# A state-space scan and a feed-forward with PReLU on one core: one layout for all chunk pairs, and another order of the first loads

## The chip, the cores and the metric

The kernel runs on one core of a Trainium2 chip. The metric is the device time in microseconds of one execution. The median of three runs before the change is 359.67 us (358.67 to 361.34). A profile shows one execution: its engines are PE (TensorE, the matmuls; PEld is its weight load), DVE (VectorE), ACT (ScalarE), POOL (GpSimd) and SP (SyncE, which here only issues DMAs). All data is 32-bit floating point.

## What is computed

Two steps, the second fed with the first one's output:

```python
# x: (4, 8, 768, 32)  a: (4, 8, 768)  B, C: (4, 8, 768, 16)
for c in range(nc):                       # chunks of the sequence
    cum = np.cumsum(la, axis=-1)          # la = log(clip(a, 1e-6, 1)) of the chunk
    L = np.exp(cum[..., :, None] - cum[..., None, :]) * causal
    y_intra = np.einsum('bhij,bhjd->bhid', (Cc @ Bc.T) * L, xc)
    y_inter = np.einsum('bhin,bhnd->bhid', Cc, state) * np.exp(cum)[..., None]
    y[:, :, sl] = y_intra + y_inter
    state = decay_full * state + sum_j(B_j x_j * decay_from_j)
# bridge: y as 3072 tokens of 256
h = x @ w_in                              # 256 -> 2048
g = np.maximum(h, 0.0) + alpha * np.minimum(h, 0.0)
out = g @ w_out                           # 2048 -> 256
```

The weights come as 64-bit numbers and are turned into 32-bit ones on the chip ("conversion" below: each of 16 pieces passes ScalarE, GpSimd, VectorE and GpSimd again).

## The kernel before

The sequence is cut into chunks of 128 tokens (Q), six to a batch element. Chunks go in pairs, twelve in all (NP); two pairs make a group of 512 tokens (GC chunks, GT tokens), and the feed-forward works by group. The order of the work is written out by hand: each engine executes its instructions in the order of the program, and a DMA is issued in the order of its queue (SP's, and ScalarE's for a few).

Per pair there are five kinds of work. **Loads**: B, C and x as tokens on the partitions (`nat`, `xt`), the running product of a for each chunk (`ap`, later `pf`), and the decay rows spread over the partitions (`abc`), which come from device memory (`scratch`), where `rows_out` stores the clamped rows (`z`) and their running products (`pf`). **Turning** B and C so that heads and states lie on the partitions (`bc`): by TensorE transposes and a ScalarE copy for pairs 0 to 4 (L640, L807), by one block transpose of VectorE for later ones (L545), whose data comes in blocks (L209). **Decays**: scans on VectorE along the tokens (`dec`), from `abc` or, for pairs 0 and 1, from rows that TensorE spreads from `ap` and `a1` (L499, L511). **Gram**: C times B (L713, L702, L822), multiplied into `dec` on VectorE (L724). C is first multiplied by `par`, which keeps even or odd heads (`cz`). **Output and state**: the new state is the old one times the decay plus B'x (`added`, L600, L831; in halves L589), masked by head on GpSimd (`sm`); y is the state times the decayed C (L768, L870; L750) plus `dec` times x (L776, L878; L758), copied to `xT` by ScalarE.

There are two layouts. Pairs 0 to 5 (`gp < HALF`) keep each chunk on all 128 partitions, and TensorE works with 128 rows of x and tiles of 128 columns. Pairs 6 to 11 put chunk k on half k of the partitions (64 tokens at a time, `SQ` = 192 columns of decay per head for both chunks), so that the two chunks' matmuls use different quarters of the array and the part above the diagonal is left out; the state products of the other half of heads need their operands on the other half of the partitions (`shifted`).

Pairs 0 and 1 are written out in `first_two`, interleaved with the conversion of the first weight pieces. `hidden_two` (L1011) is the feed-forward of the first four hidden blocks, two at a time, by halves of 256 tokens; then a loop over f from 4 to 15 takes 512 tokens at once (`hidden`, L996; `output`, L1034), with pairs 2 and 3 between, and after it 20 `quad` steps (L1120, L1095) do groups 1 to 5 by a scheme of seven products, with the later pairs between them. `keep_warm` (L326) is filler: matmuls whose result is not used.

Of the kernel before, what the change touches and what calls it, by code (L numbers as in the profile page):

```python
# [9 lines left out]
F32 = mybir.dt.float32  # L10
# [12 lines left out]
def kernel(  # L23
# [47 lines left out]
    WARM = 8  # L71
# [8 lines left out]
    HALF = NP // 2  # L80
# [9 lines left out]
    lda = ctx.enter_context(tc.tile_pool(name="lda", bufs=3))  # L90
# [48 lines left out]
    def load_tokens(dst, src, t0):  # L139


        d = dst.rearrange("p j (h w) -> p j h w", h=H)
        for k in range(2):
            for j in range(2):
                t = t0 + k * Q + j * HQ
                nc.sync.dma_start(out=d[HQ * k : HQ * (k + 1), j],
                                  in_=src[:, t : t + HQ, :].rearrange("h p w -> p h w"))

    def load_spread(gp, b, c):

        for w, t in enumerate(loads["p", gp][1] if gp >= HALF else ()):
            rows = scratch["z", b // 2].rearrange("(b h c) t -> b c h t", b=2, h=H)
            for k in range(2):
                nc.sync.dma_start(
                    out=t[HQ * k : HQ * (k + 1), : 4 * SQ].rearrange("p (h t) -> p h t", h=4),
                    in_=rows[b % 2, c + k, 4 * w : 4 * w + 4].unsqueeze(0)
                    .to_broadcast([HQ, 4, SQ]))
        for k, t in enumerate(loads["p", gp][1] if gp < HALF else ()):
            rows = scratch["z", b // 2].rearrange("(b h c) t -> b c h t", b=2, h=H)[b % 2, c + k]
            nc.sync.dma_start(out=t.rearrange("p (h t) -> p h t", h=H),  # L160
                              in_=rows.unsqueeze(0).to_broadcast([P, H, Q]))

    def load_pair(gp, decays=True):


        b, c = divmod(2 * gp, CPB)
        turned = gp > GC
        nat = ldx.tile([P, 3, 2, H * N], F32, name="nat")
        xt = ldx.tile([P, 2, HD], F32, name="xt")

        ap = ldx.tile([P, 2 * Q], F32, name="ap")
        if gp == 0:
            load_a(ap, b, c)
        elif gp >= NB:
            rows = scratch["pf", b // 2].rearrange("(b h c) t -> b h (c t)", b=2, h=H)
            rows = rows[b % 2, :, c * Q : (c + 2) * Q]
            nc.sync.dma_start(out=ap, in_=rows.unsqueeze(1).to_broadcast([H, N, 2 * Q]))
        if gp == 0:
            load_rows(0, nc.scalar)
            nc.sync.dma_start(out=al_n, in_=moe_alpha.rearrange("(k p) -> k p", p=P))  # L180
        abc = []
        later = []
        if gp >= HALF:
            load_tokens(nat[:, 0], B[b], c * Q)
        for k in range(2 if gp < HALF else 0):
            ts = slice((c + k) * Q, (c + k + 1) * Q)
            for i, src in enumerate((B,) if turned else (B, C)):
                nc.sync.dma_start(out=nat[:, i, k].rearrange("p (h n) -> p h n", h=H),  # L188
                                  in_=src[b, :, ts, :].rearrange("h p n -> p h n"))

            def load_x(k=k, ts=ts):
                nc.sync.dma_start(out=xt[:, k].rearrange("p (h d) -> p h d", h=H),
                                  in_=x[b, :, ts, :].rearrange("h p d -> p h d"))

            if gp < NB:
                later.append(load_x)
            else:
                load_x()
        for load_x in later:
            load_x()  # L200
        if gp == 0:
            loads["a", 1] = prep.tile([P, 2 * Q], F32, name="a1")
            load_a(loads["a", 1], b, c + 2)
        for i, src in enumerate((B, C) if turned else ()):


            for e in range(2):
                first = src[b, e : e + 1, c * Q : (c + 2) * Q, :]
                nc.sync.dma_start(out=nat[:, 1 + e, i],  # L209
                                  in_=bass.AP(tensor=first.tensor, offset=first.offset,  # L210
                                              ap=[[2 * S * N, P // 32], [8 * N, 32], [1, 8 * N]]))
        for k in range(2 if gp >= NB else 0):
            abc.append(lda.tile([P, H * Q], F32, name="abc"))
        loads["p", gp] = nat, abc, xt, ap
        if gp >= HALF:
            load_tokens(xt, x[b], c * Q)
        if decays:
            load_spread(gp, b, c)

    def load_second():  # L220

        rows = scratch["pf", 0].rearrange("(b h c) t -> b h (c t)", b=2, h=H)
        nc.sync.dma_start(out=loads["p", 1][3], in_=rows[0, :, 2 * Q : 4 * Q].unsqueeze(1)
                          .to_broadcast([H, N, 2 * Q]))

    al_n = const.tile([NF, P], F32, name="al_n")
    load_pair(0)
# [95 lines left out]
    def keep_warm(to, n, cols=2 * Q):  # L323

        for i in range(n):
# [6 lines left out]
    ident_h = const.tile([P, H * Q], F32, name="ident_h")  # L332
    nc.vector.tensor_copy(out=ident_h.rearrange("p (h t) -> p h t", h=H),
                          in_=ident.unsqueeze(1).to_broadcast([P, H, Q]))
# [12 lines left out]
    nc.gpsimd.tensor_tensor(out=hmask, in0=hmask, in1=bmask[:, P:], op=ALU.add)  # L347
    zeros = const.tile([P, Q], F32, name="zeros")
    nc.gpsimd.memset(zeros, 0.0)
# [46 lines left out]
    def halve_identity():  # L396

        for s in range(2):
            nc.scalar.copy(
                out=ident_p[0][HQ:].rearrange("p (a s t) -> p s a t", a=2, s=2)[:, s],  # L400
                in_=ident[HQ:, HQ * (1 - s) : HQ * (2 - s)].unsqueeze(1).to_broadcast([HQ, 2, HQ]))

    def rows_swapped():

        prs = prep.tile([RW, Q], F32, name="rpf")
        for h in range(2):
            nc.scalar.copy(out=prs[:, HQ * h : HQ * (h + 1)],
                           in_=held["pr"][:, HQ * (1 - h) : HQ * (2 - h)])
        held["prs"] = prs

    def rows_clamp(i):
        rows = loads.pop(("r", i))
        d0 = prep.tile([RW, SQ], F32, name="r0")
        nc.vector.tensor_scalar(out=d0[:, :Q], in0=rows, scalar1=1e-6, scalar2=1.0,
                                op0=ALU.max, op1=ALU.min)
        if i:
            nc.vector.tensor_scalar(out=d0[:, Q + 1 :], in0=rows[:, HQ + 1 :], scalar1=1e-6,
                                    scalar2=1.0, op0=ALU.max, op1=ALU.min)
        held[i] = d0

# [9 lines left out]

    def rows_out(i):


        d0 = held.pop(i)[:, : SQ if i else Q]
        rpf = prep.tile([RW, Q], F32, name="rpf")
        nc.vector.tensor_tensor_scan(out=rpf, data0=d0[:, :Q], data1=zeros[:RW], initial=1.0,
# [6 lines left out]
    def rows_turn(i, pr):  # L443
# [8 lines left out]
        if i == 0:  # L452
            nc.scalar.copy(out=t, in_=ps[:, :RW])
# [7 lines left out]
        if i == 0:  # L461
            nc.scalar.copy(out=alpha, in_=ps[:, RW : RW + NF])
# [978 lines left out]
```

## Time and profile before

| | us |
|---|---|
| median of three runs | 359.67 |
| the profiled execution | 359.9 |
| its span, first to last instruction | 358.2 |
| TensorE matmul busy | 350.5 |
| VectorE, ScalarE, GpSimd busy | 239.9, 173.8, 205.4 |

The first group's feed-forward starts at 17.77 us (first half of its tokens) and 24.76 us (second half), the loop over f at 28.69, the first quad at 78.96. Busy time of TensorE is modelled at the ends of matmuls, since these overlap; starts are exact. A row of the profile names a line of the kernel, the engine, the operation, the tile written and the tiles read, the shapes, the count, the busy time and the mean of one; then the idle time of the engine before it and what ended it. A line of a helper stands for all its callers.

### The profile page before, as it was taken

The numbers are of one execution on the slowest core, as the hardware profiler recorded it, in microseconds if no ns is written. First come the engines' busy times: TensorE is split into PE (matmuls) and PEld (weight loads), VectorE is DVE, ScalarE is ACT, GpSimd is POOL, SyncE is SP. The second block draws the span as 40 slices with busy tenths as digits, with TensorE's granted clock in tenths as the row PEclk, the third lists the DMA queues.
The fourth block names the chain that finished last, engine by engine and source line by source line (L and its number), as shares of the span: only waits on it lengthen the run. The fifth ranks groups of instructions, "written<-read, shape, count | busy, mean of one in ns | idle before, by whom it ended". The sixth has DMA issues, their size and how long they took to land.

```text
span 358.2 us, 7528 instructions
## 1 busy us (share of the span) xinstructions
PE 350.5 (98%) x2878; PEld 288.3 (80%) x2878; DVE 239.9 (67%) x466; ACT 173.8 (49%) x386; POOL 205.4 (57%) x222
## 2 busy tenths in 40 slices
PE   8899999999999999999999999999999999999994
PEld 8676665578788788888888888888888888888883
DVE  6987986998748756857647847757847533654272
ACT  3577666535356346346246345345445343444330
POOL 4876568589939755725655725646726544632521
PEclk9999999999999999999999999999999999999999
DMA  6989999608255403403513413413001002002003
GB/s 110 182 186 303 326 198 258 140 17 176 88 98 118 94 2 76 102 2 88 92 30 85 79 48 79 89 41 73 1 4 29 0 2 31 0 2 30 0 15 77
DMA packets 105453, 30.19 MB, mean 84 GB/s; under 512 B 79864, under 2 KB 101320, under 8 KB 105416
## 3 DMA queue, kind: packets, MB, share of 16 engines
q1 hardware_dynamic: 104488, 29.45, 37.2%
q8 instruction: 23, 0.38, 0.5%
q10 hardware_dynamic: 928, 0.25, 0.3%
q14 instruction: 14, 0.11, 0.1%
HBM read 26.32 MB, written 3.37 MB: 83 GB/s over the span
## 4 chain that ended last, share of the span: by engine, by line
PE 92%; SPq 3%; DMA 1%; DVE 1%; issue 1%; ACT 1%; POOLq 0%
PE bank L1095 34%; PE hp L1120 28%; PE bank L1034 8%; PE hp L996 6%; PE ss L1120 6%; SPq L188 2%; PE hp L1011 2%; PE ss L758 1%; PE ss L702 1%; DMA nat<-in_C_dram 1%; PE ss L750 1%; PE ss L776 1%; PE ss L713 1%; PE ss L589 1%; PE ss L768 0%
## 5 line engine op out<-in xcount | busy, mean ns | idle before, releaser
L1177 POOL TENSOR_TENSOR gt<-gt 128x512 f32<-128x512 f32 x58 | 74.1, 1277 | 21.1 <-DVE gt L1105 16.3
L1095 PE MATMUL bank<-gt,w_out 128*128 128x256 f32 x320 | 83.5, 381 | 0.0
L1095 PEld LDWEIGHTS bank<-gt,w_out 128*128 128x128 f32 x320 | 60.1, 190 | 9.2 <-issue 1.0
L1105 DVE SCALAR_TENSOR_TENSOR gt<-hp,s_mul,gt 128x256 f32<-128x256 f32 x96 | 42.0, 479 | 29.0 <-ACT gt L1103 26.8
L1167 POOL TENSOR_TENSOR gt<-gt 128x512 f32<-128x512 f32 x20 | 25.4, 1269 | 62.6 <-DVE gt L1105 57.2
L1095 PE MATMUL bank<-gt,ws 128*128 128x256 f32 x240 | 59.5, 379 | 0.0
L1103 ACT ACTIVATE gt<-hp,s_alpha 128x256 f32<-128x256 f32 x96 | 40.3, 471 | 34.5 <-PE hp L1120 31.4
L1095 PEld LDWEIGHTS bank<-gt,ws 128*128 128x128 f32 x240 | 45.6, 190 | 6.2
L1120 PE MATMUL hp<-xs,w_in 128*128 128x256 f32 x160 | 41.9, 384 | 0.0
L1120 PE MATMUL hp<-xs,ws 128*128 128x256 f32 x160 | 41.1, 380 | 0.0
L1146 DVE TENSOR_TENSOR hp<-hp,u 128x512 f32<-128x512 f32 x20 | 14.0, 699 | 35.8 <-ACT u L1144 35.8
L1120 PEld LDWEIGHTS hp<-xs,ws 128*128 128x128 f32 x160 | 30.3, 190 | 4.3 <-POOL xs L1075 0.2
L1120 PEld LDWEIGHTS hp<-xs,w_in 128*128 128x128 f32 x160 | 29.7, 190 | 4.5
L1034 PE MATMUL bank<-w_out,gt 128*128 128x256 f32 x128 | 31.0, 384 | 0.0
L1034 PEld LDWEIGHTS bank<-w_out,gt 128*128 128x128 f32 x128 | 23.6, 190 | 6.5 <-issue 3.1
L1120 PE MATMUL ss<-xT,w_in 128*128 128x256 f32 x96 | 24.6, 379 | 0.0
L996 PE MATMUL hp<-xT,w_in 128*128 128x512 f32 x48 | 22.7, 596 | 0.2 <-DVE gt L1023 0.2
L616 POOL TENSOR_TENSOR sm<-state,bmask 128x256 f32<-128x256 f32 (+1 forms) x10 | 6.2, 617 | 29.0 <-DVE state L613 29.0
L532 DVE TENSOR_TENSOR_SCAN dec<-abc,bank 128x192 f32<-128x192 f32 x48 | 22.6, 522 | 0.0
L1135 ACT COPY m<-hp 128x512 f32<-128x512 f32 x8 | 4.7, 586 | 35.7 <-PE hp L1120 35.7
L1144 ACT COPY u<-hp 128x512 f32<-128x512 f32 x20 | 11.7, 585 | 19.4 <-PE hp L1120 19.4
L1105 DVE SCALAR_TENSOR_TENSOR gt<-c,s_mul,gt 128x256 f32<-128x256 f32 x40 | 20.6, 555 | 0.0
(201 smaller groups left out, 609.6 us busy)
## 6 DMA issues: line engine op xcount, KB each, us to landing
abc<-z SPq DMA_DIRECT2D x24, 192.0 KB
raw<-in_moe_w_in_dram SPq DMA_DIRECT2D x8, 512.0 KB
raw<-in_moe_w_out_dram SPq DMA_DIRECT2D x8, 512.0 KB
abc<-z SPq DMA_DIRECT2D x8, 512.0 KB
out_dram<-o_sb SPq DMA_DIRECT2D x32, 64.0 KB
nat<-in_B_dram SPq DMA_DIRECT2D x26, 64.0 KB
nat<-in_C_dram SPq DMA_DIRECT2D x24, 64.0 KB
xt<-in_x_dram SPq DMA_DIRECT2D x12, 128.0 KB
```

What stands on the lines that cost most here:

```text
L188: nc.sync.dma_start(out=nat[:, i, k].rearrange("p (h n) -> p h n", h=H), in_=src[b, :, ts, :].rearrange("h p n -> p h n"))
L532: nc.vector.tensor_tensor_scan(out=dv[:, o : o + SQ], data0=abc[k][:, s : s + SQ], data1=ident_p[0][:, :SQ], initial=0.0, op0=ALU.mult, op ...
L996: nc.tensor.matmul(hp, w_in[:, k, f * P : (f + 1) * P], xts[g][:, k], start=(k == 0), stop=(k == KC - 1))
L1034: nc.tensor.matmul(pos[0][t // 2][:, t % 2], gt[:, t * Q : (t + 1) * Q], w_out[:, f], start=(f == 0 and t % 2 == 0), stop=(f == NF - 1), s ...
L1095: nc.tensor.matmul(ms[g][i][:, h], w, blocks[g, z][n][:, p], start=(q == 0 and h == 0), stop=(q == NQ - 1), skip_group_check=True)
L1103: nc.scalar.mul(o[:, p], h[:, p], s_alpha[:, fs[p]])
L1105: nc.vector.scalar_tensor_tensor(out=o[:, p], in0=h[:, p], scalar=s_mul[:, fs[p]], in1=o[:, p], op0=ALU.mult, op1=ALU.max)
L1120: nc.tensor.matmul(to[:, p], w(2 * z + p), b, start=start and p == 0, stop=True, skip_group_check=True)
L1144: nc.scalar.copy(out=u2, in_=A)
L1146: nc.vector.tensor_tensor(out=Y, in0=Y, in1=u2, op=ALU.add)
L1167: nc.gpsimd.tensor_tensor(out=tc_, in0=g22, in1=g12, op=ALU.subtract)
L1177: eng.tensor_tensor(out=o, in0=x0, in1=x1, op=ALU.subtract)
```

## The change

- Pairs 0 to 5 take the layout of pairs 6 to 11; the old layout's code is gone (`HALF`, `halve_identity`, `rows_swapped`, `spread`, the first form of `added`). `rows_turn` writes both halves of the partitions by four matmuls. In pairs 2 and 3 the gram comes ahead of the state sums.
- The first pair's B and C are loaded in blocks and turned by VectorE; its B is loaded as tokens too. These B loads are issued on ScalarE's queue. Pairs 1 to 4 are turned by TensorE as before.
- The second pair's decay rows come from `scratch` (`z1`), by one DMA after `rows_out`, in place of loading a again (`a1`) and clamping it.
- In `first_two`: the rows are clamped on GpSimd, the fillers are gone but for six at the start (`WARM`), the second weight piece is converted after pair 0's outputs, and loads have another order.

The core of the diff:

```diff
-    WARM = 8
+    WARM = 6
-    lda = ctx.enter_context(tc.tile_pool(name="lda", bufs=3))
+    lda = ctx.enter_context(tc.tile_pool(name="lda", bufs=2))
+    def load_blocks(nat, i, src, t0, eng=nc.sync):
+        for e in range(2):
+            first = src[e : e + 1, t0 : t0 + 2 * Q, :]
+            eng.dma_start(out=nat[:, 1 + e, i],
+                          in_=bass.AP(tensor=first.tensor, offset=first.offset,
+                                      ap=[[2 * S * N, P // 32], [8 * N, 32], [1, 8 * N]]))
+    def load_heads(dst, key, b, c):
+        rows = scratch[key, b // 2].rearrange("(b h c) t -> b h c t", b=2, h=H)
+        rows = rows[b % 2, :, c : c + 2].rearrange("h c t -> h (c t)")
+        nc.sync.dma_start(out=dst, in_=rows.unsqueeze(1).to_broadcast([H, N, dst.shape[1]]))
+    def load_first():
+        nat, _, xt, ap = pair_tiles(0)
+        load_a(ap, 0, 0)
+        load_rows(0, nc.scalar)
+        load_blocks(nat, 1, C[0], 0)
+        load_blocks(nat, 0, B[0], 0, nc.scalar)
+        load_tokens(nat[:, 0], B[0], 0, eng=nc.scalar)
+        load_tokens(xt, x[0], 0, (0,))
...
     def spread_rows(z):
         ts = [bank(r) for r in range(4)]
+        for e in range(2):
+            for r in range(4):
+                rs = slice(32 * r, 32 * r + 32)
+                row = 32 * r + N * e
+                for k in range(2):
+                    nc.tensor.matmul(ts[r][HQ * k : HQ * (k + 1), e * SQ : (e + 1) * SQ],
+                                     ident[rs, row : row + 1].to_broadcast([32, HQ]), z[rs, k],
+                                     start=e == 0, stop=True, tile_position=(32 * r, HQ * k),
+                                     skip_group_check=True)
...
         sp = spread_rows(z0)
         pr = rows_scan(0)
+        rows_product(0)
+        rows_ends(0, nc.gpsimd)
         rows_out(0)
+        load_tokens(xt0, x[0], 0, (1,))
+        load_heads(z1.rearrange("p k t -> p (k t)"), "z", 0, 2)
+        nc.sync.dma_start(out=al_n, in_=moe_alpha.rearrange("(k p) -> k p", p=P))
+        load_next()
+        nat1, _, xt1, pf1 = pair_tiles(1)
+        load_chunks(nat1[:, 1], C[0], 2 * Q)
+        load_tokens(nat1[:, 0], B[0], 2 * Q)
+        load_heads(pf1, "pf", 0, 2)
+        load_tokens(xt1, x[0], 2 * Q)
...
+        bc0 = turn_blocks(nat0)
+        rows_turn(0, pr, spare())
+        cz = czp.tile([P, 2, 2, Q], F32, name="cz")
+        spread_c(bc0, 0, nc.scalar)
+        spread_c(bc0, 1, nc.gpsimd)
+        bn0 = pair_loads(0)
+        scans(0, sp, (0,))
...
-        hp = spare()
-        keep_warm(hp, 6, Q)
...
-        convert_a(*pieces[1])
-        outputs(0, (ss(), ss()), (None, sm0[0][:, 0]), cd0, xt0, (1, 0), 2)
+        y = [ss()[:, : 2 * Q].rearrange("p (w t) -> p w t", w=2) for k in range(2)]
+        sp = spread_rows(z1)
+        nc.tensor.transpose(sp[0][:, 2 * SQ : 2 * SQ + NF], al_n, ident[:NF, :NF])
+        state_products(y, (None, sm0[0][:, 0]), cd0)
+        x_products(y, xt0, dec[0], (False, True), (1, 0))
+        nc.scalar.copy(out=alpha, in_=sp[0][:, 2 * SQ : 2 * SQ + NF])
+        copy_out(0, y)
+        slopes(alpha)
...
+        convert_a(*pieces[1])
+        scans(1, sp, (0, 1))
...
-    load_next(2)
-    rows_clamp(0)
+    load_next()
+    rows_clamp(0, nc.gpsimd)
...
-    beside[GC] = m5_bank[0][:, : 2 * Q]
+    beside[GC] = m5_bank[0], ss_tile()
```

## The prediction

> **What bounds the kernel now.** I read the busy table first, then the chain of waits, then the chain's first 45 us in order of time, then rows by operation.
>
> ```profile
> PE 350.5 (98%) x2878; PEld 288.3 (80%) x2878; DVE 239.9 (67%) x466; ACT 173.8 (49%) x386; POOL 205.4 (57%) x222
> PE 92%; SPq 3%; DMA 1%; DVE 1%; issue 1%; ACT 1%; POOLq 0%
> ```
>
> TensorE holds 92% of the chain that ended last; from 28.69 on it never pauses: a window over 28.69 to 60 us reads 31.31 busy of 31.31, one over 100 to 340 reads 240.00 of 240.00. So the end is the time at which this dense stretch begins, plus TensorE's own work in it. What VectorE, ScalarE or GpSimd save after 28.69 is hidden. Before 28.69 the chain is made of waits:
>
> ```profile
> 13.06 3.57 DMA nat<-in_C_dram
> 16.67 0.34 PE hp L807
> 17.04 0.59 ACT bc L810
> 17.77 1.97 PE hp L1011 x8
> ...
> 24.33 0.38 ACT xT L883
> ...
> 24.76 2.01 PE hp L1011 x8
> ...
> 28.69 1.95 PE hp L996 x4
> ```
>
> (Start, length, what.) The second pair's last C chunk lands at 16.63; only then can TensorE turn it, and everything to 24.76, where the second half of the first group enters the feed-forward, follows from it.
>
> **What the skill says.** "DMA: Bandwidth & Descriptors", section "Why a DMA increments its semaphore by 16 and not by 1": a load runs on the largest number of engines, at most 16, that divides the slowest dimension of both sides. A block load's source has 4 outermost, a head-broadcast's 8: so 4 and 8 engines. The trace agrees for blocks, which before loads only for later pairs (four issued at L209 from 82.35 to 84.68):
>
> ```profile
> 82.00:84.00 2.00, 2.00 (x11) 1.75 (x10) 1.38 (x3) 1.02 (x3) 1.92 (x3) 1.00 1.14 133
> 84.00:86.00 2.00, 2.00 (x11) 1.75 (x10) 1.97 (x5) 1.19 (x4) 2.00 (x3) 1.00 0.31 79
> ```
>
> (Window, length, busy time of PE, PEld, DVE, ACT, POOL, clock, DMA share, GB/s.) With blocks alone in flight the share falls to 0.31, five engines of 16, and 79 GB/s: four blocks of 64 KB need 256 KB / 79 = 3.3 us.
> Same page, "Issuing engines are not separate DMA queues": a second queue saves issue time only. Before has just one load on ScalarE's queue, so no run here shows it.
> "TensorE: Matmul & The Clock Gate", Part 1: half clock at the start and after about 3.4 us without work. The trace agrees on the start: the 16 filler instructions of L326 at 0.83 take 3.68 us (230 ns each), the 12 at 7.23 take 1.5 us (125 ns).
>
> **Part 1: matmuls of pairs 2 to 5** (in the dense stretch) take the form that pairs 6 to 11 have already, so both prices are in the trace.
>
> ```profile
> 62.00:65.00 3.00, 1.15 (x16) 0.72 (x16) 1.00 1.12 155
> ...
> 227.00:230.00 3.00, 0.91 (x32) 0.59 (x32) 1.00 0.33 80
> ```
>
> These are the gram matmuls alone, L713 (old form) and L702 (new): busy 1.15 against 0.91. From first start to the next matmul of other lines: old gram 63.05 to 64.12 = 1.07, new 200.80 to 201.63 = 0.83. Outputs: old 49.96 to 51.57 = 1.61 with state products of both chunks, 71.35 to 72.74 = 1.39 with one; new, with the next pair's 32 state instructions, 207.01 to 208.76 = 1.75. Old state sums 55.60 to 55.96 = 0.36 (two chunks), 0.25 (one); new about 0.46 and 0.35, so new outputs are 1.75 - 0.46 = 1.29. Pair 2: 1.07 + 1.61 + 0.25 = 2.93 becomes 0.83 + 1.29 + 0.35 = 2.47. Pair 3: 2.82 becomes 2.58. Pairs 4 and 5 as pairs 3 and 2 but with both chunks' products: 3.04 to 2.58, 2.93 to 2.47. Sum 0.46 + 0.24 + 0.46 + 0.46 = **1.6 us off the path**.
> Beside it, hidden by this dense TensorE: each pair's scans go from 8 x 664 ns (L538) to 8 x 522 (L532), its products from 4 x 680 to 4 x 550 (L724); added are two ScalarE copies (297 ns, L661) and up to two GpSimd copies (287 ns, L663), which put about 1 us ahead of a weight conversion that in pair 2 ends at 48.76 for a use at 53.96. Its decays shrink from 1 MB to 768 KB. If that cover went, a late conversion would show at once as TensorE idle. One new wait I do charge: pair 4's state sums now also use an "ss" buffer, which the first quad's Z takes two allocations later; Z (78.96 before) must wait for VectorE's L613 (78.70 to 79.29): **0.3 us**, from 0 to 0.5.
>
> **Part 2: the start.** Removed: the wide identity (0.77 us, not waited for), 8 filler instructions of the first 16, 12 at 7.23 and 4 at 13.32, the spread's second form (L511, 2.61 us), the four transposes of pair 0. Its four scans shrink from 1203 to an estimated 900 ns (384 columns for 512), 1.2 us together. Added to VectorE: a block transpose (1.1 us, L545), placed before those scans in its order. What decides is when the blocks land. `ap` (128 KB on eight engines: 0.8 us at twice the blocks' rate) lands by 3.73 (VectorE clamps it then before). Four block loads share four engines with it: from about 2.4, 0.8 + 3.3 gives 6.5, and 0.8 to landing (C's packets end near 15.9 for the landing at 16.63) is 7.3; token loads from the second queue mix in, so I take 7.8, ends 5 and 8.5.
> Then, by adding up: turned 8.9; first scan 9.8, pf 10.2, three scans 12.9 (11.01 before). C's two spreads run on ScalarE (0.5) and GpSimd (1.06, the price of L486) to 10.0, gram to 10.9 (10.09 before).
> Meanwhile the queues: loads signal eight semaphores in turn, and each waits for the landing of the eighth before it. In the built order the store of z on SP waits for the last C block (7.8), z1 for z's landing (raw weights of 512 KB go ahead of it: 10.2), and z1 itself, 192 KB on 8 engines, lands near 13.9. The last B load of pair 1 waits for z1's semaphore, so pair 1's B is complete near 18.0, not 16.63; behind it on SP stand pf1, x and the next weights. On ScalarE's queue the fourth B token load waits for the first C block, and the table load and the prt copies stand behind it (to 8.9, still before they are needed).
> TensorE has z1's spread ahead of pair 0's outputs: spread 15.0, outputs 16.4 (15.78 before), two xT copies 17.3, and only then the second weight piece's conversion (ahead of them before): ScalarE 18.6, GpSimd's clip 18.65, VectorE 19.35, GpSimd's w_in 20.7, cd 21.4, mask 21.85, ScalarE's three half moves 22.3 (0.3 each, new), PReLU 23.15, gram copy 23.6, GpSimd's product 24.6, outputs 25.6; ScalarE is then at 26.05 with conversion and PReLU, and the copies, now split by token so that both are needed, end at 26.85. Against 24.76 this is **2.1 us later**, ends -1.0 (blocks at 5, z1 at 11.5, pair 1's loads in time) and +5 (below). From there the order of work to the dense stretch is as before.
>
> **Sum:** -1.6 + 0.3 + 2.1 = +0.8. The profiled execution took 359.9 for a span of 358.2, 0.2 above the median of 359.67; so 360.7 against it, 360.5 for the median. That is no change by the bound of 1% (3.6 us), about what a measurement of this kernel can tell. The case's own range is 358 to 362.
>
> **Rivals.** (a) *The clock stays at half* and it ends slower. Place: TensorE between rows_turn (ends about 6.3: z's spread starts at 4.5 as before, estimated 1.3, and 0.5 for the turn) and the gram of pair 0 (10.0), 3.7 us without the filler that before ran there. It decides if this gap passes the 3.4 us of the skill's page, or if six first fillers don't raise the clock at all. Price: gram and sums 1.2, spread 1.0, outputs 1.4 doubled, 3.6 less what other waits cover (about 1), plus half of the first feed-forward (1.9): about +3.5, so 364. For it: the gap as I date it; against: an earlier landing of the blocks closes it. Chance 0.25.
> (b) *The loads are early.* Blocks land at 5, z at 8.5, z1 at 11.5; then z1 isn't waited for long and pair 1's landing sets the end as before, but near 16: start 0.2 later to 1 us earlier, 357.3 to 358.5. To be faster by over 1% the start must give another 1 us or more. For it: two queues keep the engines filled; against: share 0.31 for blocks. Chance 0.25, a third of it beyond 1%.
> (c) *It doesn't do what it says in pairs 2 to 5*: moved halves or late states stall TensorE and the 1.6 is lost, 362. Against: pairs 6 to 11 run dense in this form. Chance 0.1.
> The likeliest case has 0.4. Range 357 to 364.5: it holds cases (b) and (c) nearly whole and most of (a). Faster by over 1% 0.1, slower 0.27 (most of (a), a little of (c)), same 0.63.
>
> **What would show it.** Right: the block transpose starts at 7 to 8, not 5; z1's spread near 14; the second half's feed-forward near 26.9 and the dense stretch from about 30.8; gram 0.83 in pairs 2 to 5. (a) shows as matmuls of the first 18 us at twice their lengths of before (the clock column reads 1.00 even where the fillers take 230 ns, so lengths decide). Wrong if the dense stretch starts before 28, or has gaps after it.

## The result, and the profile after

The changed kernel takes **369.96 us** (369.65 to 371.2, six runs) against 358.99 (358.45 to 361.34, six runs): 1.030 times the time before, 95% interval 1.027 to 1.033, slower by 11 us. The forecast of 360.5 and its range up to 364.5 were both too low. The profiled execution took 370.06 us with a span of 368.3.

The busy table and the shares of the chain that ended last, as they were shown of before:

```profile
PE 350.8 (95%) x3235; PEld 287.4 (78%) x3235; DVE 229.8 (62%) x468; ACT 175.2 (48%) x401; POOL 210.4 (57%) x232
PE 74%; SPq 11%; DMA 8%; DVE 2%; issue 1%; POOL 1%; ACT 0%; ACTq 0%; POOLq 0%; DVEq 0%
```

TensorE's work is the same to 0.3 us (350.5 before), but its share of the chain fell from 92% to 74%, and SyncE's queue (SPq) and DMAs hold 19%. So the chain now runs through the issue and landing of loads. Starts of the same work in both profiled executions show where:

| start of | before | after | later by |
|---|---|---|---|
| gram of pair 0 | 10.09 | 10.19 | 0.10 |
| first half's feed-forward | 17.77 | 21.66 | 3.89 |
| second half's feed-forward | 24.76 | 30.60 | 5.84 |
| first quad | 78.96 | 90.50 | 11.54 |
| a late product of the last quad (`hp<-xT,ws`) | 339.97 | 351.55 | 11.58 |

Half of the loss arises before 30.60 us, half in the loop over f (5.70), and nothing after it. (The span grew by only 10.1, since the tail after that product is 1.5 shorter.) The chain of waits in order of time (start, length, what) names the queue that feeds both stretches:

```profile
2.42 5.38 DMA nat<-in_B_dram
8.37 3.44 DMA z<-r
...
13.51 1.84 SPq L151
15.40 0.58 SPq L151
16.02 1.15 SPq L145
17.22 0.64 SPq L145
17.90 0.63 SPq L145
18.57 0.63 SPq L145
...
36.80 9.83 DMA raw<-in_moe_w_in_dram
46.65 2.00 SPq L145
...
58.52 7.65 DMA abc<-z
...
90.50 1.13 PE ss L1010 x4
```

L145 is the new token load. One pair's B is now four loads of 64 partitions where it was two of 128, and so is its x; SyncE issues them back to back, 0.61 to 0.64 us each, no quicker than a load of 128 partitions (L151, 0.58). Some issues are held longer, such as the 1.84 and 1.15 above; by what, is not shown. The row of pair 2's B below shows four in 3.69 us. Windows of the start (length, busy time of PE, PEld, DVE, ACT and POOL, clock, DMA share, GB/s), in which mostly loads of B, C and x are in flight and no weights:

```profile
18.00:21.00 3.00, 2.03 (x64) 1.51 (x52) 1.82 (x3) 1.43 (x4) 1.58 (x3) 1.00 0.49 59
30.00:33.00 3.00, 2.40 (x11) 2.14 (x12) 2.35 (x4) 2.51 (x7) 1.96 (x2) 1.00 0.70 61
```

and one of before with chunk loads (its last us has two weight pieces as well; 24 to 26 alone reads 0.74 and 97):

```profile
24.00:27.00 3.00, 2.94 (x38) 2.36 (x27) 2.90 (x5) 2.58 (x6) 1.69 (x3) 1.00 0.86 106
```

The DMA engines have room (share 0.49 and 0.70, some 60 GB/s where before moved 97) while the queue is full: here the issue of loads is short, not bandwidth. Later it is the other way: from 42 to 54 us, with the delayed weights in flight, the share is 1.05 to 1.08. Another limit could have held the queue: the issue records name eight semaphores in turn, and at 45.60 and 46.65 an issue went out only when the load before it on its semaphore had landed (45.54 and 46.63). But from 12 to 43 us every issue's semaphore had been free for 1.3 us or more, so in the start that limit did not bind.

What waits for it, and two other waits that the forecast did not have, stand in the timeline of after (start, length, engine, line, what; in brackets the idle time before it and what ended it):

```profile
15.38 1.58 PE L465 MATMUL bank<-z,ident 32*64 32x192 f32 x32 [2.11 <-DMA z<-z]
...
20.96 0.48 PE L498 MATMUL hp<-ident,nat 128*128 128x128 f32 x1 [0.20 <-DMA nat<-in_B_dram]
...
21.66 2.94 PE L901 MATMUL hp<-xT,w_in 128*128 128x256 f32 x8
24.62 0.61 ACT L733 COPY moved_c<-cd 64x128 f32<-64x128 f32 x2 [1.14 <-POOL cd L839]
25.26 3.69 SPq L145 DMA_DIRECT2D nat<-in_B_dram  x4
30.60 3.72 PE L901 MATMUL hp<-xT,w_in 128*128 128x256 f32 x16 [1.14 <-ACT xT L753]
...
42.51 1.98 PE L886 MATMUL hp<-xT,w_in 128*128 128x512 f32 x4 [0.42 <-POOL w_in L306]
45.40 1.99 PE L924 MATMUL bank<-w_out,gt 128*128 128x256 f32 x8 [0.91 <-POOL w_out L306]
...
68.67 0.60 ACT L631 COPY moved_c<-cd 64x128 f32<-64x128 f32 x2 [3.33 <-POOL cd L628]
...
71.15 0.75 DVE L890 SCALAR_TENSOR_TENSOR gt<-hp,s_mul,gt 128x512 f32<-128x512 f32 x1 [2.15 <-ACT gt L889]
71.95 0.43 PE L536 MATMUL hp<-cz,bc 32*64 32x256 f32 x2 [0.63 <-DVE gt L890]
...
90.50 0.70 PE L1010 MATMUL ss<-xT,w_in 128*128 128x256 f32 x2 [1.80 <-DVE state L594]
```

**The start** adds up from these rows. TensorE turns the last part of pair 1's B at 20.96, where in before it turned the last C chunk at 16.67: +4.29. From there to the first feed-forward 0.70 for 1.10: -0.40. That feed-forward takes 2.86 to the gram behind it for 1.89, by slow matmuls: +0.97. (The clock records of the trace begin with full clock at 23.77 in after and at 6.10 in before. Ahead of the first record the clock column reads 1.00, but the lengths of the matmuls are those of half clock.) Gram and second feed-forward -0.19. Outputs to second half 2.91 for 1.74, of which 1.14 is TensorE's wait for ScalarE's xT copies: +1.17. Sum +5.84.

**The loop** pauses three ways. Weights come late behind the token loads (42.51, 45.40: TensorE waits for the converted pieces). At 68.67 ScalarE has stood 3.33 us before a copy `moved_c`, which waits for GpSimd's product `cd`; PReLU, VectorE and pair 3's gram follow it (2.10 us from its start to the sums, for 0.84 without a pause). At 90.50 the first quad waits 1.80 for VectorE's states to leave the "ss" buffer.

### The profile page after: what moved, and what is told of

The parts are those of the page before. It is cut to its first block, busy times and chain, and to the rows that moved or that the text cites. A ratio compares the mean times of both kernels' runs of the same rounds, so it can differ in the third digit from the quotient of the medians.

```text
span 368.3 us, 8299 instructions
## 1 busy us (share of the span) xinstructions
PE 350.8 (95%) x3235; PEld 287.4 (78%) x3235; DVE 229.8 (62%) x468; ACT 175.2 (48%) x401; POOL 210.4 (57%) x232
## 4 chain that ended last, share of the span: by engine, by line
PE 74%; SPq 11%; DMA 8%; DVE 2%; issue 1%; POOL 1%; ACT 0%; ACTq 0%; POOLq 0%; DVEq 0%
PE bank L985 33%; PE hp L1010 28%; SPq L145 6%; PE ss L1010 6%; SPq L151 3%; DMA raw<-in_moe_w_in_dram 3%; DMA abc<-z 2%; PE bank L924 2%; PE ss L556 2%; PE ss L536 2%; DMA nat<-in_B_dram 1%; PE ss L681 1%; DMA z<-r 1%; SPq L237 1%; DMA nat<-in_C_dram 1%
## 5 line engine op out<-in xcount | busy, mean ns | idle before, releaser
L995 DVE SCALAR_TENSOR_TENSOR gt<-hp,s_mul,gt 128x256 f32<-128x256 f32 x96 | 42.0, 479 | 30.8 <-ACT gt L993 27.0
L480 DVE TENSOR_TENSOR_SCAN dec<-abc,bank 128x192 f32<-128x192 f32 x80 | 37.8, 527 | 1.0 <-DMA abc<-z 1.0
L1010 PEld LDWEIGHTS hp<-xs,w_in 128*128 128x128 f32 x160 | 29.7, 190 | 4.5
L521 POOL TENSOR_TENSOR sm<-state,bmask 128x256 f32<-128x256 f32 (+1 forms) x13 | 8.1, 620 | 30.4 <-DVE state L594 28.3
L1010 PEld LDWEIGHTS ss<-xT,w_in 128*128 128x128 f32 x96 | 18.2, 190 | 4.5 <-DVE state L594 2.0
```

Of the source, the lines that this page charges most:

```text
L480: nc.vector.tensor_tensor_scan(out=dec[:, h], data0=abc[:, h * SQ : (h + 1) * SQ], data1=ident_p[0][:, :SQ], initial=0.0, op0=ALU.mult, op ...
L995: nc.vector.scalar_tensor_tensor(out=o[:, p], in0=h[:, p], scalar=s_mul[:, fs[p]], in1=o[:, p], op0=ALU.mult, op1=ALU.max)
L1010: nc.tensor.matmul(to[:, p], w(2 * z + p), b, start=start and p == 0, stop=True, skip_group_check=True)
```

## The experiments

Each has its own before on the same chip; the ratios are to that. The theories at first: too many loads for SyncE (called T1 in the expectations), the clock without its fillers (T2), and the way of the second pair's a through device memory; later the Z buffer and ScalarE's copies (T5). The medians of e5, e9, e10 and e15 ended above the range given for their repair, that of e13 below it.

### Loads: the count alone (e1), whole loads (e9), another order (e4), another queue (e6)

e1 is the kernel before with only B and x of pairs 1 to 4 cut in two loads of 64 partitions each:

```diff
-                nc.sync.dma_start(out=xt[:, k].rearrange("p (h d) -> p h d", h=H),
-                                  in_=x[b, :, ts, :].rearrange("h p d -> p h d"))
+                for ps in halves(gp, True):
+                    nc.sync.dma_start(out=xt[ps, k].rearrange("p (h d) -> p h d", h=H),
+                                      in_=x[b, :, ts, :][:, ps].rearrange("h p d -> p h d"))
```

> The kernel before with nothing changed but this: each load of a B or x chunk of pairs 1 to 4 is issued as two loads of 64 partitions, so these pairs issue 13 loads as the changed kernel does (9 before), with the same bytes and descriptors; TensorE's work, fillers and waits on other engines are those of before. Theory T1 (SyncE takes 0.6 us for each issue whatever its size, so more and smaller loads leave the DMA engines short and the weights late): SyncE issues 16 more loads in the first 80 us, 10 us of issue time; the second half's feed-forward starts at 26 to 29 (24.76 before) and TensorE pauses between 30 and 60; 362 to 366 in all. Theory T2 (the loss comes from the half clock of the first 23 us, or from the changed form of the pairs): no change, 359 +- 1.

It took 362.44 us for 358.6: 1.011 (1.009 to 1.012), +3.8 us by the count of loads alone. Its second half starts at 25.14, only 0.38 later and ahead of the 26 to 29 expected; the loop takes the rest (57.29 for 54.20). The window from there to 60 us of e1, which in before holds no pause from 28.69 on:

```profile
25.14:60.00 34.86, 32.73 (x207) 20.58 (x208) 26.19 (x43) 22.12 (x44) 21.42 (x23) 1.00 0.87 232
```

TensorE is idle 2.13 of 34.86. The cover "hidden by this dense TensorE" is gone with nothing changed but the number of loads.

e9 is the other direction: the changed kernel with B and x of pairs 1 to 4 in two loads of 128 partitions. It leaves out the placing of the tokens on the halves that the products expect, so this and the later kernels with whole loads (e10, e11, e13, e14, e16, e17) show what the loads cost, and are no kernels to use.

```diff
+        for k in ks if whole else ():
+            t = t0 + k * Q
+            eng.dma_start(out=d[:, k], in_=src[:, t : t + Q, :].rearrange("h p w -> p h w"))
-        load_tokens(nat[:, 0], B[b], c * Q)
+        load_tokens(nat[:, 0], B[b], c * Q, whole=gp <= GC)
```

> The changed kernel with B and x of pairs 1 to 4 loaded in two loads of 128 partitions each instead of four of 64: same bytes and same number of descriptors, half the issues; the tokens then stand on other partitions than the products expect, so these pairs' results are other numbers (every instruction and its size is that of the changed kernel). Theory T1 (number of loads): SyncE saves 4 x 0.65 = 2.6 us a pair; pair 1's B lands at 19 to 20 for 20.96, the second half's feed-forward starts at 28.5 to 29.7, the pauses from 40 to 76 (about 4.3 us) go, only the first quad's wait stays: total 363.5 to 366. Theory T2 (form of the pairs, clock, GpSimd): 368.5 to 370.

366.92 us, 1.023 (1.020 to 1.026). The same stretch of e9, and the two stretches of after:

```profile
29.43:60.00 30.57, 30.36 (x246) 20.57 (x247) 24.36 (x43) 21.81 (x45) 21.37 (x24) 1.00 0.98 247
```

```profile
30.60:60.00 29.40, 27.79 (x230) 17.70 (x231) 21.70 (x41) 18.88 (x38) 17.57 (x20) 1.00 0.88 210
60.00:90.50 30.50, 27.67 (x265) 18.04 (x263) 21.73 (x40) 15.47 (x33) 23.44 (x25) 1.00 0.66 144
```

The pauses up to 60 us are gone (0.21 idle for 1.61, and 247 GB/s for 210). Those at pair 3 and before the first quad stay. The Trainium skill, "Perfetto Trace Analysis", section "DMA Optimizations", has two remarks that pull apart here: smaller DMAs may let some start sooner, and a bottleneck of descriptor generation is met by balancing. Splitting cost 3.8 us in e1, and joining gained 3 in e9; in neither did the second half start sooner with the smaller loads.

e4 puts pair 2's x behind seven weight pieces and the decays:

```diff
-            load_tokens(xt, x[b], c * Q)
+            if gp != NB: load_tokens(xt, x[b], c * Q)
...
+        if f == FIRST: load_tokens(loads["p", NB][2], x[0], 2 * NB * Q)
```

> The changed kernel with the four loads of pair 2's x (used at 50.5) moved behind the next seven weight pieces and pair 2's decays in SyncE's order; nothing else. Theory T1 (in the loop the weights are late because SyncE is still issuing token loads): the weight piece issued at 34.24 goes out at 31.6, ScalarE's wait of 3.4 us for it shrinks to under 1.5, TensorE's pauses between 40 and 50 (0.6 at 40.2, 1.2 at 42.5) go, total 367.7 to 369. If the loop's pauses come from VectorE, ScalarE and GpSimd having more to do: pauses stay, total 369.5 to 370.5.

369.4 us, 1.031 (1.029 to 1.033), against 1.030: nothing. Pair 2's gram starts 2.51 earlier (46.53 for 49.04, 0.65 of it from an earlier start); then pair 2's sums of B'x waited for the late x (gram to sums paused 1.6), and a clock episode (below) took the rest. Another order shares the shortage out anew; it does not end it.

e6 issues x of pairs 1 and 2 from GpSimd, four loads in the start and four later:

```diff
+        load_tokens(xt1, x[0], 2 * Q, eng=nc.gpsimd)
...
+        load_tokens(loads["p", 2][2], x[0], 4 * Q, eng=nc.gpsimd)
```

> The changed kernel with the eight token loads of x of pairs 1 and 2 issued by GpSimd (four in its pause after 5 us, four after 15 us) instead of SyncE; same bytes, same descriptors, same number of loads, only the issuing engine differs. Theory T1a (SyncE's issue time is the chain): SyncE saves 8 x 0.65 = 5.2 us by the time it reaches pair 2's decays; pair 2's loads start 2.6 us earlier, the next weight piece goes out at 29 for 34.24, the second half's feed-forward starts 0.5 to 2 us earlier, the pauses from 40 to 53 (2.5 us) go: total 366 to 368. Theory T1b (the DMA engines or the eight semaphores are the limit, whoever issues): total 369 to 370.5. If GpSimd's own issue takes over 1 us a load, cz and the conversions get later and it ends above 371.

372.08 us, 1.036 (1.034 to 1.039), worse. The pauses from 40 to 53 went, as SyncE then had eight loads fewer, and the loop takes 57.01 for 59.90; but the second half starts 3.2 later (33.83). Two rows of its timeline:

```profile
4.87 3.00 POOL L145 DMA_DIRECT2D xt<-in_x_dram  x4
...
11.93 0.62 POOL L452 TENSOR_TENSOR bn<-nat,prt 128x256 f32<-128x256 f32 x1 [1.54 <-DMA nat<-in_B_dram]
```

Four issues hold GpSimd for 3.00 us, and then GpSimd waits 1.54 for the first pair's own B, which is in flight beside them. The Trainium skill, "DMA: Bandwidth & Descriptors", section "Issuing engines are not separate DMA queues", says that a second issuer saves only the time of issuing; in the loop it did. In the start, its own time and the earlier place of what it sends cost more.

### The first quad's buffer (e5, e10)

```diff
-    beside[GC] = m5_bank[0], ss_tile()
+    beside[GC] = m5_bank[0], bank(2)
```

> The changed kernel with one buffer chosen differently: the second half of pair 4's state sums goes to bank 2, free at that time, instead of an ss buffer, so the first quad's Z no longer takes a buffer that VectorE has still to read. If that choice makes the wait of 1.97 us ahead of the first quad (88.5 to 90.5): Z starts right after the turns at 88.5, nothing else moves, total 367 to 368.3 (more if the wait also drops the clock in some runs). If VectorE's delay alone makes it (Z waits for something else next): 369.5 to 370.5.

> The run with whole loads and, in addition, pair 4's sums in the free bank 2. If the two costs are separate, 2 us less than with whole loads alone: 361.5 to 364; if the wait ahead of the first quad has gone with the loads: the same within 0.5.

e5 took 368.71, 1.027 (1.025 to 1.029). e10 is e9 with this line: 364.92, 1.017 (1.015 to 1.019), 2.0 below e9 in the same set of runs. In e5's timeline the first quad follows the turns at once:

```profile
88.58 0.38 PE L500 MATMUL ss<-ident,nat 128*128 128x128 f32 x2
88.80 1.03 PE L1010 MATMUL ss<-xT,w_in 128*128 128x256 f32 x4
```

The wait that the forecast put at 0.3 is worth 2.0 with whole loads (e10), and 1.2 alone (e5), where the intervals of e5 and after overlap.

### Clock and the way through device memory (e2, e3)

e2 puts fillers back (two more at the start, twelve instructions before pair 0's gram and twelve before z1's spread):

```diff
-    WARM = 6
+    WARM = 8
+        keep_warm(gram[2], 6, Q)
...
+        keep_warm(y[0].rearrange("p w t -> p (w t)"), 6, Q)
```

> The changed kernel with fillers put back: 16 filler instructions at the start as before, 12 ahead of the first gram in the gap from 6.9 to 10.2, 12 in the gap from 13.3 to 15.4. Theory T2 (half clock makes the late start): the first spread, the first gram and the first feed-forward take 0.8, 0.85 and 1.9 for 1.52, 1.52 and 2.87; the second half's feed-forward starts at 28 to 28.7 for 30.60, total 367.5 to 368.5. Theory T1 (the loads are late): the matmuls get shorter as well, but the next waits (z1's landing at 15.3, pair 1's B at 20.96, the conversions) take up most of it; feed-forward at 29.8 to 30.6, total 369 to 370.

369.93 us, 1.031 (1.027 to 1.035). The matmuls did quicken (gram of pair 0 took 0.84 for 1.52, the first feed-forward 1.84 for 2.86), yet the second half started at 30.21, only 0.4 earlier, and half clock behind the pause before the first quad took 1.7. The slow clock is real; in this profile the landing of pair 1's B set the first feed-forward again (22.12 for 20.92 in after). But e2 does not price the whole of it: its clock records show full clock from 4.30 to 11.12 only, then half clock to 17.95, and the second group of fillers itself, at half clock, kept TensorE from 14.12 to 16.97, past z1's landing at 15.27:

```profile
14.12 2.93 PE L314 MATMUL ss<-const-float32-1.0 128*128 128x128 f32 x12
16.97 1.34 PE L465 MATMUL bank<-z,ident 32*64 32x192 f32 x32
```

e3 loads the second pair's a from the input, and GpSimd clamps it:

```diff
+        load_a(loads["a", 1], 0, 2)
-        load_heads(z1.rearrange("p k t -> p (k t)"), "z", 0, 2)
+            nc.gpsimd.tensor_scalar(out=z1[:, :, o], in0=a1[:, :, t], scalar1=1e-6, scalar2=1.0,
+                                    op0=ALU.max, op1=ALU.min)
```

> The changed kernel with the second pair's a loaded straight from the input behind the first x loads, as before, and clamped by GpSimd, in place of the load of z from device memory, which waits for z's store to land (SyncE at 11.88, landing 15.3). If the round through device memory is a main part of the late start: the second spread starts at 13.3 for 15.38, SyncE reaches pair 1's loads 1.2 to 1.9 us earlier, the second half's feed-forward starts at 28.5 to 29.2 for 30.60, total 368 to 368.7. If pair 1's loads or the clock set the start whatever z1 does: 30 to 30.6 and 369.4 to 370.

369.86 us, 1.032 (1.030 to 1.034). The second half starts 0.99 earlier and the first quad's stretch is reached 2.7 earlier, and then 1.9 is given back behind it. Half-microsecond windows of e3 (the number before the last two is the clock):

```profile
87.00:87.50 0.50, 0.00 (x0) 0.00 (x0) 0.40 (x3) 0.00 (x0) 0.49 (x1) 1.00 0.12 35
...
88.50:89.00 0.50, 0.50 (x4) 0.39 (x3) 0.50 (x2) 0.00 (x0) 0.50 (x1) 0.70 0.12 39
89.00:89.50 0.50, 0.50 (x3) 0.41 (x2) 0.50 (x3) 0.40 (x1) 0.50 (x2) 0.50 0.55 195
...
92.00:92.50 0.50, 0.50 (x4) 0.45 (x3) 0.00 (x0) 0.00 (x0) 0.50 (x2) 0.89 0.30 39
```

TensorE paused from 86.00 to 87.82; from 88.71 to 92.12 the clock was at half, which costs at most half of these 3.41 us.

### Combinations, and the wait that was still missing (e7, e8, e11)

e7 joins e3, e6 and e5; e8 adds fillers. e11 is e10 with the fillers, the straight a, and whole loads for pair 0 too.

> Three edits together: the second pair's a straight from the input, x of pairs 1 and 2 issued by GpSimd, and the free bank for pair 4's sums. If the three causes add up: second spread at 13.5 to 14, second half's feed-forward at 27.5 to 29 for 30.60, no pause over 0.7 from 34 to 90 except the one of pair 3's gram, total 362.5 to 365. If each only uncovers the next wait: 366 to 368.

> The same three edits with fillers as well: 16 filler instructions at the start and 12 ahead of the first gram. If the half clock costs anything once the loads are early: first gram 0.84 for 1.52, second spread 0.84, first feed-forward 1.9 for 2.9, 1 to 2 us less than the run without the fillers (361 to 364). If it is covered by other waits: the same time within 0.7 us.

> Whole loads for pairs 0 to 4 (again other numbers in these pairs), the second pair's a straight from the input, the free bank, and fillers (16 at the start, 12 ahead of the first gram): what is left of the change is the form of pairs 0 to 5 and the block turn. If these four account for the loss: second half's feed-forward at 25 to 27, no pause over 0.7 after it, total 356.5 to 359.5, at or below the kernel before, since pairs 2 to 5 take 1.4 less. If a cause is missing: 361 to 364.

e7 took 370.39 (1.032, 1.030 to 1.034), e8 370.93 (1.034, 1.032 to 1.036): e6's late start outweighs the others. e11 took 364.61 (1.017, 1.013 to 1.022), hardly below e10 and well above what it was expected to reach. With loads, buffer and a repaired and the fillers back, 6 us were still missing, so a cause was. The timeline of e11 gave it:

```profile
24.35 0.60 ACT L738 COPY moved_c<-cd 64x128 f32<-64x128 f32 x2 [2.33 <-POOL cd L849]
...
26.88 0.45 PE L751 MATMUL bank<-moved_c,moved_s 64*32 64x128 f32 x14 [0.65 <-ACT moved_s L738]
```

ScalarE stands 2.33 us before the copies that move `cd` to the other half, and all that it does later stands behind them.

### ScalarE's copies later in its order (e12, e13)

```diff
-        for k in range(2):
-            moved("c", k, cd1[:, k])
...
-        moved("s", 0, sm0[1][:, 0])
...
         decayed(heads_of(dec[1], 0), g0, nc.gpsimd)
+        for k in range(2):
+            moved("c", k, cd1[:, k])
+        moved("s", 0, sm0[1][:, 0])
```

and likewise in the generator of the later pairs: the two copies stand behind the PReLU of the step (`move_c`). e12 does this to the changed kernel, e13 to e11.

> The changed kernel with the ScalarE copies of cd (moved_c) of pairs 1, 2 and 3 placed later in ScalarE's order: in pair 1 behind the copy of the first gram, in pairs 2 and 3 behind the gram products; number and size of all instructions unchanged. Theory T5 (ScalarE stands still until GpSimd has cd, 1.1 us in pair 1, 1.9 in pair 2, 3.3 in pair 3, and with it the feed-forward's activations and the conversions queued behind): the pause in pair 3's gram (2.10 for 0.84) and the one behind it (2.39 for 1.73) go, 1.9 us, and the second half's feed-forward starts 0.5 to 1.5 us earlier: total 366.5 to 368. If ScalarE's wait is covered: 369 to 370.5.

> The run of all but the form (whole loads in pairs 0 to 4 with other numbers in these pairs, second a straight, free bank, fillers), and the late copies of cd on top. T5: the same 2.5 to 3.5 us come off there, where the loads are on time: second half's feed-forward at 27.7 to 28.5 for 29.46, pair 3's gram dense, total 361 to 362.5. Otherwise 364 to 365.

e12: 369.97, 1.030 (1.026 to 1.035), no gain. Pair 3's gram follows without its pause (0.92 for 2.10), and its loop is 1.60 shorter than in after; but in its profiled execution the second half started 1.3 later, TensorE waited for weights to 44.08 and 46.97 (0.70 and 0.91), and half clock followed the pause before the first quad. e13: **360.53 us** (359.94 to 362.3, 20 runs), 1.004 (1.0025 to 1.0056): 4.1 below e11, of which these two profiles have 2.47 in the start and 1.91 in the loop. Its chain shares and its windows:

```profile
PE 91%; POOL 2%; ACT 2%; DMA 1%; DVE 1%; issue 1%; ACTq 0%; POOLq 0%; DVEq 0%
```

```profile
27.00:60.00 33.00, 32.80 (x255) 22.39 (x256) 25.53 (x45) 24.27 (x49) 23.11 (x25) 1.00 1.00 264
60.00:80.14 20.14, 20.14 (x238) 13.45 (x237) 18.92 (x32) 9.85 (x20) 15.72 (x17) 1.00 0.48 71
```

TensorE is dense to the first quad again. One table puts the steps in order:

| kernel | second half starts | first quad starts | between |
|---|---|---|---|
| before | 24.76 | 78.96 | 54.20 |
| after | 30.60 | 90.50 | 59.90 |
| e9: whole loads | 29.43 | 86.45 | 57.02 |
| e10: and free bank | 29.91 | 84.98 | 55.07 |
| e11: and fillers, straight a | 29.46 | 84.52 | 55.06 |
| e13: and late copies | 26.99 | 80.14 | 53.15 |

In this order of repairs the loop's loss is 2.88 by the loads, 1.95 by the buffer, 1.91 by the copies. Without them the loop is 1.05 shorter than before. Another order shares it out anew: e15 below keeps the split loads, and its loop of 54.78 is 1.63 above that of e13.

### What the start still costs (e14 to e17)

e16 is e13 without fillers, e17 e13 with z1 from device memory again, e14 e13 with the second pair's a and both x loads of pair 0 ahead of the first weights, and GpSimd's clamp of that a ahead of its part of C's spread:

```diff
-        load_tokens(xt, x[0], 0, (0,), whole=True)
...
         load_a(loads["a", 1], 0, 2)
+        load_tokens(xt, x[0], 0, whole=True)
```

e15 has these repairs except whole loads, and pair 2's x at the end of the start's loads.

> The run with whole loads and late copies of cd (360.5; other numbers in pairs 0 to 4) with the change's own fillers, 12 instructions at the start and none later. If the half clock costs what rival (a) says, now that other waits are gone: first gram 1.52 for 0.84, first feed-forward 2.5 to 2.9 for 1.92, 1 to 3 us more, 361.5 to 363.5. If it is covered even here: 360 to 361.

> The run with whole loads and late copies of cd (360.5; other numbers in pairs 0 to 4) with the second pair's z read back from device memory as the change does. If the round trip costs by itself: second spread at 14 to 15 for 13.1, SyncE's loads of pair 1 behind it 0.5 to 1.5 later, 0.7 to 2 us more, 361.2 to 362.5. If it is covered: 360 to 361.

> As the run before, and the second pair's a and both x loads of pair 0 are issued ahead of the first weight piece, a clamped by GpSimd in its pause before cz (other numbers in pairs 0 to 4 again). If the rest of the late start is the order of the first loads: second spread at 12.5 to 13.3 for 14.56, second half's feed-forward at 26 to 27.3, total 359 to 361, near the kernel before. If the path from the gram on sets it: less than 0.7 us off.

> The changed kernel with every repair that keeps its result: second a and x of pair 0 first, fillers, late copies of cd, free bank, pair 2's x behind its decays; token loads stay in four parts. Off 369.9: bank 2.0, copies of cd 1.9 to 3, start 1 to 2, pauses from 40 to 47 1.5 to 2.5: 361.5 to 364, still above the kernel before because of the token loads. At 359 or below the token loads would not matter.

e16: 361.27, 1.006 (1.004 to 1.008), +0.7, with intervals that overlap; second half at 28.61. e17: 362.36, 1.010 (1.006 to 1.014), +1.8; second half at 29.13. In both, and in e14, the loop takes 53.15 as in e13. e14: 361.07, 1.006 (1.004 to 1.008), no gain: pair 0's x came in time, but its gram later, 11.71 for 10.11, as GpSimd's clamp waited for a until 8.88 with C's spread behind it. e15: 366.26, 1.020 (1.017 to 1.023), 3.7 below after, and still 2% slower than before: with four loads for each B, pair 1's B is waited for 3.8 us and the second half starts at 31.54.

```profile
21.18 0.45 PE L501 MATMUL hp<-ident,nat 128*128 128x128 f32 x1 [3.82 <-DMA nat<-in_B_dram]
```

e15 and e14 differ only in the split of the loads and the place of pair 2's x. Between them lie 5.2 us of the median; in the profiles the start is 4.11 later (31.54 for 27.43) and the loop 1.63 longer. So with all else repaired the number of loads is the largest single cause, in the start more than in the loop. No version beat the kernel before.

Starts differ from execution to execution: e5 changes nothing before the first quad, and its second half started at 32.16 for 30.60 in after. So 1 or 2 us of one profile's start are no evidence; the medians are, and so the +1.3 of e12's start is not explained.

## Why the prediction was wrong

**Held.** The blocks landed at 7.80 (forecast 7.8) and were turned from 8.00; gram of pair 0 began at 10.19 (forecast to end at 10.9, at 0.83 for the form: 10.07); where nothing paused, gram in the new form took 0.84 (0.83). e13, which takes away the three waits of the loop, restores the fillers and loads a straight, starts its second half at 26.99 (26.9), its dense stretch at 30.92 (30.8) and takes 360.53 (360.5). In after itself the grams of pairs 2 and 3 were paused and took 1.50 and 2.10. So the forecast describes another kernel than the one that ran, and the agreement in numbers is luck: e13 lacks z1's round trip (1.8 in e17), which the forecast did price, and its clock records show half clock from 11.82 to 18.65, over z1's spread and pair 0's outputs (13.09 to 17.19), which the forecast had at full clock. The two errors offset each other. The landing of the blocks is partly luck too: the window that the forecast read as blocks alone (share 0.31) also held token loads, which landed until 85.00, and the decay loads issued from 84.73.

At the first quad the forecast had +1.7 (2.1 for the start, 0.70 less in the loop, 0.3 for Z) and after has +11.54. Of the 9.84 between them 3.74 arose in the start and 6.10 in the loop with Z.

**"Hidden by this dense TensorE"** is the step that failed most. I costed the new copies and the later conversions at nothing, and for the case that the cover goes I named the sign (a late conversion shows as TensorE idle) but worked out no price. Two things broke the cover. The loads of pairs 1 to 4 went from two to four per tensor, which I never counted at SyncE: 2.88 us of the loop, shown by e9, and from the other side 3.09 by e1. And I priced the copies by their own 0.3 us, not by what they wait for: ScalarE stood 3.33 us for `cd` with PReLU behind it, 1.91 in the loop and 4.1 in all (e13 against e11).

**"2.1 us later"** was 5.84. The failing term is pair 1's B "complete near 18.0": it landed at 20.92. z was stored by 11.81 for 10.2, so z1 landed at 15.24 for 13.9. But the wait that I had, of the last B load for z1's semaphore, was not what bound: that load went out at 18.57, 3.3 us after z1 had landed. SyncE's own time was: seven other issues stand between z1's and it (11.88 to 18.57, two C chunks and three B loads among them), and 2.35 from issue to landing followed. The slow first feed-forward, 0.97, was rival (a) come true in part: fillers gave 0.4 in the start and nothing in the median (e2), as loads were later; with loads and copies repaired they are worth 0.7 (e16), not resolved. ScalarE's late xT copies I had (1.14 us of TensorE's wait; outputs at 25.6 and copies at 26.85 in the forecast, 1.25). z1's round trip is worth 1.8 in the median once nothing else is later (e17), and 0.1 alone (e3).

**"0.3 us, from 0 to 0.5"** for the first quad's Z was 1.97. I dated VectorE's states by their time in before, relative to Z. In after VectorE comes to them at 89.79 and 90.16, behind the next rows' products, which the chain has from 85.63 to 89.08. That this order is what makes them late is read from the chain; e10 shows the size.

**"1.6 us off the path"** was mis-sized: in the loop 1.05 (e13; forecast 0.70 for pairs 2 and 3), but after it nothing: pairs 4 and 5 had 0.92 coming, and the time from the first quad to the late product of the table is 261.05 for 261.01. In e13 it is even 0.5 longer than before, which gives back half of the loop's gain. Part of it is `rows_turn` of the second batch, which I had not costed: four matmuls (eight instructions) in 0.49 for two transposes in 0.17. The rest was not traced.

**The rivals.** (b) did not come. (a) came: its condition that six first fillers do not raise the clock held, since full clock begins at 23.77 in after. Most of its price was covered by later loads (e2), and the 0.7 of e16 is all that was measured; no run holds full clock through the whole start, so what that would give is open. (c) had the right mechanism, "moved halves or late states stall TensorE": 1.91 and 1.95 us, but I gave it 0.1, because the later pairs run dense in this form, and a price of only the lost 1.6. The later pairs have their loads and rows long before; these have not. No rival was "more loads on one queue", though the change's new token loads show it. Not settled: why starts vary by up to 1.6 us, what holds single issues for 1 to 2 us, and how the missing gain of pairs 4 and 5 was lost.

## What to carry to other kernels

Count the DMA issues of each queue before and after, at their measured 0.4 to 0.6 us each, before asking about bytes: a layout that halves a load's partitions doubles its cost on the issuing engine, and everything behind it in that queue, weights too, comes later. Price a new copy on an in-order engine by the time at which its operand is ready, with what stands behind it, not by its own length. When one repair gives nothing, look for the wait that took its place and repair both in one kernel: here whole loads, a buffer and an order of copies gave 0 to 3 us each alone and 9.4 together with the fillers and the straight load.

## What the runs showed of the hardware

- A load from SyncE held its queue 0.63 us with 512 descriptors and 0.58 with 1024 where nothing held it longer; with mostly the former in flight (18 to 21 us of after), the DMA engines had a share of 0.49 and moved 59 GB/s. Four such issues from GpSimd held it for 3.00 us (e6).
- All nine kernels that start with 16 filler instructions have full clock on record from 4.3 to 6.9 us, all ten with 12 only from 18.8 to 29.7 us. In every record a stretch of half or full clock lasts a multiple of 3.41 us (3.41, 6.83, 10.24 and so on); only the last one, which the end of the span cuts, does not.
- Half clock followed short pauses. The Trainium skill, "TensorE: Matmul & The Clock Gate", Part 1, gives about 3.4 us without work; in e2, e3, e4 and e12 a pause of 1.6 to 1.8 us was followed, 0.1 to 1.7 us after its end, by 3.41 us at half clock. In after, e6 and e9 the same pause of 1.8 us before the first quad kept full clock. What decides it stays open; a pause need not last 3.4 us.
- Such episodes gave back what an experiment had gained (in e3 1.9 of 2.7 us), so a repair's gain is to be read from the ledger of starts, not from the total alone.
